# Gated linear attention into a squared-ReLU FFN: output sums scaled in PSUM and copied by ScalarE, turns placed one by one

## The chip, the cores and the metric

The kernel runs on 1 core of one Trainium2 chip. The metric is the device time of one execution in microseconds (us); less is better. Times named here are medians of several runs, or belong to one execution that was recorded by the profiler.

## The reference

The first part is a recurrent attention with a gate, the second a feed-forward network with a squared ReLU. Everything is float32.

```python
def _attn_ref(q, k, v, alpha):             # (4, 8, 768, 48) each
    for t in range(S):
        state = alpha[:, :, t, :, None] * state + np.einsum('bhd,bhe->bhde', k[:, :, t], v[:, :, t])
        y[:, :, t] = np.einsum('bhd,bhde->bhe', q[:, :, t], state)

x = attn_out.transpose(0, 2, 1, 3).reshape(3072, 384)
h = np.maximum(x @ w_in, 0.0)              # w_in (384, 2048)
out = (h * h) @ w_out                      # w_out (2048, 384)
```

## The kernel before

**Attention.** The 768 steps of each of the 4 batches are cut into 6 chunks of 128; a chunk of one batch, with its 8 heads, is a block, and there are 24 blocks. Blocks are worked on in pairs, named by the even block (`n0`): logarithms of alpha (`ln`, ScalarE), split of these into two parts (`sp`, VectorE), running sums over the chunk (`cs`, TensorE), exponentials of the sums (`eb`, `ei`, ScalarE), products with q and k (`mq`, `mk`, VectorE), the turn of both products (`turn`, 32 transposes for each block of TensorE into PSUM, then `kc`, `qc`, ScalarE copies), then `ga` and `gb` (scores, state sums, masks, states, and the outputs of an older pair), and at last the copies of the attention output into `x` (`ev_part`, ScalarE).

**FFN.** Four blocks make a group of 512 tokens, so there are 6 groups, `g` = 0 to 5. The first layer has 16 hidden tiles of 128 x 512 (`in_x`, `in_y`, `in_post`), the second sums 16 hidden tiles into 4 output tiles of 128 x 384 (`out_x`, `out_y`). Group 0 does most of its work in plain float32 (`ffn_in`, `out_plain`). From then on every factor is split in three: a scaled coarse part `a` or `b`, a remainder `l` and a difference `d`. Two passes, `b` times `a` and `l` times `l`, are summed in PSUM with the factor E = 2**-12 pending, and the third, `d` times `d`, is added. So a result is the first sum times (1 + E) plus the `d` pass.

For a hidden tile there are three ways to do that, one letter each in `tp` (in `tp1` for group 1). With `D`, ScalarE copies the first sum times E to `hid` (L754), VectorE adds PSUM after the `d` pass (L663) and squares with the ReLU (L771). With `M` and `A`, ScalarE scales the sum inside PSUM by 1 + E (L756) and the `d` pass is summed on top; then ScalarE does the ReLU (L776), and VectorE (`M`) or ScalarE (`A`) the square. For an output tile there is one way in groups 1 to 5: ScalarE copies the first sum times E to `osb` (L872), and VectorE adds PSUM to it after the `d` pass, and the store follows on SP's queue.

The weights' parts are made by `prepare`: `cast_w` on ScalarE, `rest_w` and `diff_w` on VectorE; `keep` stores the parts in DRAM, and `pump` fetches them again for each later group, all on SP's queue. `split_h` and `diff_h` split the hidden tiles; `splits_of_x` asks for the split of the next group's x.

**Order.** All engines run their own queue in order. The order is written by a weave: the FFN's steps are units with a cost, the attention's steps and the preparation of the weights are events with a time in the same units, and an event is put ahead of the first unit that starts at its time or later. The table `AT` holds these times; `base[g]` is where a group starts. `g0`, `g1`, `g2`, `g` list the pairs of each group: time, pair, whether it closes an older pair, whether it starts one, and for some a time at which `ga` and `gb` of the pair are done together (`joined`). `o0`, `o2`, `w_first`, `w_in_at`, `w_in_by` place the preparation of weights, `d_at` and `d_by` the differences of the output weights, `ahead` says how many steps ahead of their use the hidden tiles are split. The first 39 us follow the list `first`, which is written out.

`pads` and `places` put `align(place)` into TensorE's code: no-ops up to the slot `place` of a block of 256 instructions, at a time in a group or ahead of a pair's turn.

Of the kernel before, what the change touches and what calls it, by code (L numbers as in the profile page):

```python
# [12 lines left out]
AF = mybir.ActivationFunctionType  # L13
# [2 lines left out]


GB = 4
AT = {'v_by': (5.25, 6.24, 17.64), 'before': 2.2, 'places': ((4, 202), (16, 181)), 'pads': ((1, 9.0, 122), (1, 16.5, 223), (1, 33.0, 11), (2, 6.5, 120), (2, 21.0, 109)), 'evs': 0.65, 'lead': 4, 'lead1': 4, 'post': 3, 'w_first': (49.63, 28.64, 58.58), 'wstep': 0.45, 'd_at': 36.74, 'd_by': 0.95, 'w_in_at': 2.6, 'w_late': 1.45, 'w_in_by': 3.8, 'room1': 22, 'room': 25, 's0': 4, 'ahead': 5, 'xs': 0.2, 'g0': ((3.75, 4, False, True, 27.75), (21.38, 6, True, True), (27.75, 8, True, False)), 'sc0': (2.35, 2.35, 2.35), 'g1': ((1.38, 8, False, True, 15.62), (15.62, 10, True, True), (29.23, 12, True, False)), 'g2': ((0.56, 12, False, True), (19.11, 14, True, True), (32.13, 16, True, True)), 'g': ((1.71, 6, True, True), (17.38, 8, True, True)), 'g1x': 48.74, 'g2x': 49.24, 'gx': 46.88, 'g0x': 56.38, 'k0': 2, 'h0': 14, 'h1by': 2, 'evs0': 0.3, 'tp': 'ADMD', 'tp1': 'MMAD', 'split': 8, 'o0': (48.99, 50.24), 'o2': (17.75, 26.12, 26.5, 29.0, 30.61, 34.99), 'str1': 25.13, 'ga': 9.5, 'gb': 13.0, 'cv0': 1.5, 'first': 'ln0 warm0 cs0 load0v load2a ei0 load1v eb0 mk0 ln1 fill1 fill1 kT0 cs1 kc0 eb1 mq0 qT0 mq1 ei1 qc0 fill1 mk1 fill1 lt0 sc0 lt1 kT1 kv0 qT1 am0 ln2 weights2 us0 load2q kc1 qc1 cs2 sc1 fill1 am1 load2k ei2 load3a eb2 load4a fill1 kv1 st0 first0 us1 fill1 middle0 ln3 mq2 load3k ya0 qT2 yb0 mk2 fill1 qc2 kT2 cs3 kc2 load3q load2v weights5 sc2 eb3 load3v fill1 sga0 sgb0 fill1 ei3 ev0 mq3 mk3 am2 fill1 late0 qT3 kT3 sgc0 first1 kc3 qc3 middle1 kv2 ha0 sc3 us2 kv3 sga1 ha1 am3 us3 sgb1 load4k ya2 load4q load4v first2 yb2 late0 sgc1 middle2 weights6 ev2 lt3 lt2 st2 ha3 ha2 sgb2 sga2 hb1 sgc2 hb0 hb2 weights1 st1 hb3 st3 weights0', 'd3': 3.0}


RUN = {0: 128, 32: 32, 64: 64, 96: 32}
# [3 lines left out]
def kernel(  # L26
# [12 lines left out]
    nc = tc.nc  # L39
    B, H, S, D = q.shape  # L40
    C = 128
    NCH = S // C
    NP = H // 2
    NBLK = B * NCH
    DM, DF = moe_w_in.shape
# [49 lines left out]
    for x, n in (("q", 2), ("q", 3), ("k", 3)):  # L95
        t = lent[x, n] = two_k("qk_lent", shape=(H, 64))
# [144 lines left out]
    last = consts.tile([128, 4, NP], FP32, name="last")  # L241
# [36 lines left out]

    SPLIT = AT["split"]

# [361 lines left out]
    E = 2.0**-12  # L642
    NEAR = 1.0 - 2.0**-13
    acc = {}
# [8 lines left out]
    here, todo, room = {}, [], [22]  # L653
# [4 lines left out]
    def scaled_sum(out, x, scale, op, z):  # L658
        nc.vector.scalar_tensor_tensor(out=out, in0=x, scalar=scale, in1=z, op0=ALU.mult, op1=op)  # L659
# [7 lines left out]
    def lasting(w, p):  # L667
        return w == "o" and p < NW - AT["k0"]

# [9 lines left out]
    def keep(x, w, p):  # L679
        nc.sync.dma_start(out=kept_parts[x, w, p], in_=words(here[x, w, p]))  # L680
        stored.add((x, w, p))

    def rest_w(w, p):
        l = here["l", w, p] = wt("wl", FP32R, shapes[w])
        scaled_sum(l, whole[w][p], 1.0 / E, ALU.subtract, here["b", w, p].bitcast(FP32))
        cut.add((w, p))
        keep("l", w, p)

    def diff_w(w, p):
        l = here["l", w, p]  # L690
        d = here["d", w, p] = here.pop(("l", w, p)) if lasting(w, p) else wt("wd", FP32R, shapes[w])
        scaled_sum(d, here["b", w, p].bitcast(FP32), -E, ALU.add, l.bitcast(FP32))
        keep("d", w, p)
        pump()

    def prepare(at, w, p, late=0, diff_at=None):
        step = AT["wstep"]
        fs = (cast_w, rest_w, diff_w)
        out = [(at + i * step + late * (i > 1), f, (w, p)) for i, f in zip((0, 1, AT["d3"]), fs)]
        return out if diff_at is None else out[:-1] + [(diff_at, diff_w, (w, p))]  # L700

    def pump():
        while todo and todo[0] in stored and len(here) + 2 * NW - len(cut) < room[0]:
# [60 lines left out]
    kinds, g_now = [""], [0]  # L764
# [74 lines left out]
    def new_out(t):  # L839
        if t % 2 == 0:  # L840
            acc["out", t // 2] = cv_pool.tile([128, 2, DM], FP32, tag="upper", name="osb")
        return out_tile(t)
# [13 lines left out]
    def out_x(n, ns):  # L856
        p, jj = divmod(n, 2)
        a, l = h_parts.pop(n)
        for t in range(GB):
            if n == ns[0]:  # L860
                new_sum(t)
            of_tile(t, a, here["b", "o", p][:, jj], start=n == ns[0])
            of_tile(t, l, here["l", "o", p][:, jj], stop=n == ns[-1])
            if n == ns[-1]:
                x = acc[t][:, 0:DM]
                if len(ns) < NJ:
                    o = out_tile(t)
                    nc.vector.scalar_tensor_tensor(
                        out=o, in0=x, scalar=E, in1=o, op0=ALU.mult, op1=ALU.add
                    )  # L870
                else:
                    nc.scalar.activation(out=new_out(t), in_=x, func=AF.Copy, scale=E)  # L872
        if jj:
            used("l", "o", p)

    def out_y(g, ps, t, last):
        for p in ps:
            for n in (2 * p, 2 * p + 1):
                of_tile(
                    t, h_diff[n], here["d", "o", p][:, n % 2], stop=last and n == 2 * ps[-1] + 1  # L880
                )
        if last:
            o = out_tile(t)
            combine(((o, acc.pop(t)[:, 0:DM], ALU.add, o),))
            store(g, t, o)
        if t == GB - 1:
            for p in ps:
                h_diff.pop(2 * p)
                h_diff.pop(2 * p + 1)
                used("d", "o", p)  # L890
# [48 lines left out]
            hid[j] = two_k("hid")  # L939
        nc.scalar.activation(out=hid[j][:, cols], in_=r, func=AF.Square)  # L940

    def store(g, t, o):
        c, b = divmod(g * GB + t, B)
        r0 = (b * NCH + c) * C
        nc.sync.dma_start(out=out[r0 : r0 + C, :], in_=o)


    steps = {f.__name__: f for f in (ln, sp, cs, eb, ei, mq, mk, bl, br, lt, qT, qc, kT, kc, ev)}
# [19 lines left out]
    first = AT["first"]  # L968
    for word in first.split():
        f = max((x for x in steps if word.startswith(x)), key=len)  # L970
# [25 lines left out]
    places = dict(AT["places"])  # L996
# [5 lines left out]
    def attention(t, n0, after, scale=1, begun=True, whole_at=None, turn_at=None):  # L1002

        out = []
        old = n0 - 2 if after else None
        given = old, n0 if begun and n0 < NBLK else None

        def loads(at, *which):
            out.extend((at, load, (m, x)) for m, x in which if m < NBLK)

        for at, fs in EARLY if n0 < SPLIT else PLAN:
            for f in fs.split():
                w = t + (AT[f] if scale == 1 and f in ("ga", "gb") else at) * scale
                if f in ("ga", "gb") and whole_at is not None:
                    w = whole_at
                if f in ("turn", "kc0", "kc1", "qc0", "qc1") and turn_at is not None:
                    w = turn_at + (at - 6.5) * scale
                if f == "ga":
                    out.append((w, ga if whole_at is None else joined, given))
                elif f == "gb":  # L1020
                    if whole_at is None:
                        out.append((w, gb, given))
                    if after:
                        for p in range(NP):
                            out.append((w + AT["evs" if scale == 1 else "evs0"] * p, ev_part, (old, p)))
                if not begun:
                    continue
                if f == "ga":
                    loads(w, (n0 + 3, "k"))
                elif f == "gb":  # L1030
                    loads(w + AT["v_by"][0], (n0 + 2, "v"))
                    loads(w + AT["v_by"][1], (n0 + 3, "v"))
                    loads(w + AT["v_by"][2], (n0 + 4, "k"))
                elif n0 >= NBLK:
                    continue
                elif f == "turn":
                    if n0 in places:
                        out.append((w - AT["before"], align, (places[n0],)))
                    out.append((w, turn, (n0,)))
                    loads(w, (n0 + 2, "q"), (n0 + 3, "q"))  # L1040
                else:
                    n = n0 + int(f[-1])
                    out.append((w, steps[f[:-1]], (n,)))
                    if f[:-1] == "cs":
                        loads(w, (n + 2, "a"))
        return sorted(out, key=lambda x: x[0])
# [12 lines left out]
    NG = NBLK // GB  # L1059
# [38 lines left out]
    cv0 = AT["cv0"]  # L1098
# [11 lines left out]
    for g in range(1, NG):  # L1110
# [5 lines left out]
        if g + 1 < NG:  # L1116
            for t, n0, after, run, *other in AT["g1"] if g == 1 else AT["g2"] if g == 2 else AT["g"]:
                n0 = n0 if g < 3 else n0 + GB * g
# [46 lines left out]
```

## Time and profile before

| | |
|---|---|
| median of 3 runs | 520.47 us (519.84 to 520.86) |
| the profiled execution, its own time | 522.12 us |
| its span | 520.3 us |
| TensorE busy | 509.2 us (98%) |
| VectorE busy | 371.3 us (71%) |
| ScalarE busy | 308.8 us (59%) |

The span runs from the first to the last instruction of the profiled execution; its own time includes what lies around it. PE is TensorE's matmuls, PEld its weight loads (they overlap), DVE is VectorE, ACT ScalarE, POOL GpSimd, SP the engine whose queue issues most transfers. L739 is line 739 of the kernel. In a group of instructions, `o<-wd,hd 128x384 x288` means 288 instructions that write the tile `o` from `wd` and `hd`; what follows the bar is their busy time in us and the mean of one in ns, and after the next bar the idle time of the engine ahead of them with the engine and line that ended it.

### The profile page before, as it was taken

What the parts mean: (1) busy time and instruction counts of PE and PEld (TensorE: products, weight loads), DVE (VectorE), ACT (ScalarE), POOL (GpSimd) and SP (SyncE); (2) the same over time, 40 slices, a digit from 0 to 9 for tenths busy, and PEclk for the clock granted to TensorE, in tenths of its full rate; (3) what the DMA queues carried; (4) which work ended last, traced back from release to release, by engine and by line L of the source; (5) the groups of instructions that cost most, each with busy time, mean ns of one, the idle gap of its engine ahead of it and who ended that gap; (6) DMA issues with size and microseconds to landing.
All of it is one profiled execution on the core that took longest, in us unless ns stands there. A gap on an engine that the chain in (4) does not pass through costs nothing.

```text
span 520.3 us, 13238 instructions
## 1 busy us (share of the span) xinstructions
PE 509.2 (98%) x5382; PEld 427.1 (82%) x5382; DVE 371.3 (71%) x641; ACT 308.8 (59%) x656; POOL 32.4 (6%) x77
## 2 busy tenths in 40 slices
PE   8889999999999999999999999999999999999997
PEld 6666446669887999888998987899988899988996
DVE  3887979998997996776993566696465476363961
ACT  5577995676978656465663665954266855164620
POOL 4000202000102000010101020000000000000000
PEclk9999999999999999999999999999999999999999
DMA  9889776616889548799765689866673534798101
GB/s 174 179 241 272 216 184 143 177 33 229 246 241 199 168 116 295 251 263 274 201 169 144 205 241 266 228 171 183 234 250 124 185 121 154 274 332 301 64 1 60
DMA packets 133884, 101.58 MB, mean 195 GB/s; under 512 B 104640, under 2 KB 107712, under 8 KB 133824
## 3 DMA queue, kind: packets, MB, share of 16 engines
q1 hardware_dynamic: 132288, 100.68, 67.5%
q8 instruction: 43, 0.70, 0.6%
q0 software_dynamic: 1536, 0.05, 0.3%
q14 instruction: 17, 0.14, 0.1%
HBM read 83.39 MB, written 17.33 MB: 194 GB/s over the span
## 4 chain that ended last, share of the span: by engine, by line
PE 61%; DVE 4%; ACT 2%; DMA 1%; issue 0%; DVEq 0%
PE o L831 28%; PE h L739 26%; PE y L412 3%; PE T L590 1%; PE sckv L432 1%; PE sckv L460 1%; DVE wl L659 1%; ACT x L628 1%; DMA wl<-li 1%; ACT hx L714 1%; DVE hd L663 1%; DVE hl L659 0%; PE cs L300 0%; PE cs L301 0%; DVE q_in L316 0%
## 5 line engine op out<-in xcount | busy, mean ns | idle before, releaser
L739 PE MATMUL h<-xa,wb 128*128 128x512 f32 x240 | 68.5, 394 | 0.0
L739 PE MATMUL h<-xl,wl 128*128 128x512 f32 x240 | 67.7, 390 | 0.0
L739 PE MATMUL h<-xd,wd 128*128 128x512 f32 x240 | 67.0, 393 | 0.5 <-issue 0.5
L628 ACT COPY x<-y 32x256 f32<-32x256 f32 (+2 forms) x132 | 47.3, 365 | 24.9 <-PE y L412 22.4
L831 PE MATMUL o<-wb,ha 128*128 128x384 f32 x176 | 59.8, 340 | 0.0
L756 ACT ACTIVATE h<-h 128x512 f32<-128x512 f32 x44 | 25.8, 586 | 56.3 <-PE h L739 56.1
L831 PE MATMUL o<-wl,hl 128*128 128x384 f32 x176 | 58.9, 335 | 0.0
L831 PE MATMUL o<-wb,hx 128*128 128x384 f32 x160 | 54.2, 339 | 0.0
L831 PE MATMUL o<-wl,hx 128*128 128x384 f32 x160 | 53.6, 335 | 0.5 <-DVE hx L659 0.5
L663 DVE TENSOR_TENSOR hid<-h,hid 128x512 f32<-128x512 f32 x36 | 24.8, 688 | 40.0 <-PE h L739 37.2
L739 PEld LDWEIGHTS h<-xl,wl 128*128 128x128 f32 x240 | 45.0, 188 | 9.9 <-DVE xl L659 0.2
L739 PEld LDWEIGHTS h<-xd,wd 128*128 128x128 f32 x240 | 44.4, 188 | 9.8 <-issue 0.9
L739 PEld LDWEIGHTS h<-xa,wb 128*128 128x128 f32 x240 | 44.4, 188 | 9.2
L831 PE MATMUL o<-wd,hd 128*128 128x384 f32 x288 | 51.4, 335 | 0.0
L831 PEld LDWEIGHTS o<-wd,hd 128*128 128x128 f32 x288 | 49.9, 188 | 0.2
L931 PE MATMUL h<-x,w_in 128*128 128x512 f32 (+1 forms) x120 | 42.8, 510 | 1.5 <-DVE s L489 1.2
L754 ACT ACTIVATE hid<-h 128x512 f32<-128x512 f32 x36 | 21.6, 601 | 29.8 <-PE h L739 29.7
L714 ACT ACTIVATE ha<-hid 128x512 fp32r<-128x512 f32 x44 | 27.8, 639 | 18.6 <-DVE hx L659 8.2
L931 PEld LDWEIGHTS h<-x,w_in 128*128 128x128 f32 x120 | 22.5, 190 | 18.9 <-issue 15.1
L659 DVE SCALAR_TENSOR_TENSOR hl<-ha,hid 128x512 fp32r<-128x512 f32 x44 | 30.2, 686 | 7.1 <-ACT ha L714 7.1
L831 PEld LDWEIGHTS o<-wb,ha 128*128 128x128 f32 x176 | 33.0, 188 | 0.7
L831 PEld LDWEIGHTS o<-wl,hl 128*128 128x128 f32 x176 | 33.0, 188 | 0.3
(119 smaller groups left out, 922.8 us busy)
## 6 DMA issues: line engine op xcount, KB each, us to landing
wl<-lo SPq DMA_DIRECT2D x34, 384.0 KB, 4.5
wd<-do SPq DMA_DIRECT2D x34, 384.0 KB, 3.8
wl<-li SPq DMA_DIRECT2D x32, 384.0 KB, 4.3
wd<-di SPq DMA_DIRECT2D x32, 384.0 KB, 4.6
raw<-in_moe_w_in_dram SPq DMA_DIRECT2D x8, 768.0 KB, 6.8
raw<-in_moe_w_out_dram SPq DMA_DIRECT2D x8, 768.0 KB, 4.6
v_in<-in_v_dram SPq DMA_DIRECT2D x24, 192.0 KB, 4.5
out_dram<-osb SPq DMA_DIRECT2D x24, 192.0 KB, 2.0
```

The lines of the kernel that those rows point to most:

```text
L412: ins = nc.tensor.matmul(out=ys[e][64 * half : 64 * half + D + G * e, m % 2, p // 2, t], lhsT=lhsT, rhs=rhs, start=(half, e) not in seen, ...
L432: nc.tensor.matmul(out=ps[e][HALF[h], 0, p, :], lhsT=ks[rows, p, HALF[h]], rhs=qs[rows, p, HALF[h]], start=True, stop=True, skip_group_che ...
L460: nc.tensor.matmul(out=ps[h][64 * e : 64 * (e + 1), 1, p, G:64], lhsT=tile_of("k", n)[HALF[h], 2 * p + e, :], rhs=tiles["v"][n % NV][HALF[ ...
L628: copy(out=x[kk][to : to + m, t : t + 2], in_=blk[n]["y"][e][r : r + m, :, p // 2],)
L659: nc.vector.scalar_tensor_tensor(out=out, in0=x, scalar=scale, in1=z, op0=ALU.mult, op1=op)
L663: nc.vector.tensor_tensor(out=o, in0=x, in1=z, op=op)
L714: nc.scalar.activation(out=a, in_=x, func=AF.Copy, scale=E * NEAR)
L739: nc.tensor.matmul(out=acc["h", j], lhsT=here[w, "i", p][:, kk, jj * 128 : (jj + 1) * 128], rhs=x_parts[x][:, kk], start=start and kk == 0 ...
L754: nc.scalar.activation(out=hid[j], in_=x, func=AF.Copy, scale=E)
L756: nc.scalar.activation(out=x, in_=x, func=AF.Copy, scale=1.0 + E)
L831: nc.tensor.matmul(out=acc[t][:, 0:DM], lhsT=lhs[:, t * C : (t + 1) * C], rhs=rhs, start=start, stop=stop, skip_group_check=True,)
L931: nc.tensor.matmul(out=ps, lhsT=w[:, kk, c0 : c0 + 128], rhs=xT[g][kk][:, cols], start=(kk == 0), stop=(kk == KM - 1),)
```

## The change

- **Output sums.** A letter for each group, `'oa': 'DAAADA'`. In groups with `A` (1, 2, 3 and 5) ScalarE scales an output tile's first sum inside PSUM by 1 + E, the `d` pass is summed on top, and ScalarE copies the finished tile to `osb`. Groups 0 and 4 stay as they were.
- **The last tile** of group 5 is copied and stored in two halves of 192 columns: VectorE's half is stored by SP's queue, ScalarE's by ScalarE's own.
- **Turns.** `td` shifts the turn of each pair and its copies by a time of its own.
- **Stores of weight parts.** `keep` becomes an event of its own, `sd` later than the part that it stores (0.49 for `l`, 0 for `d`).
- **The table.** Most times of `AT` move, `tp1` goes from MMAD to MMMA, `ahead` from 5 to 4, `h0` from 14 to 16, five pads become four at other slots. The list `first` and the rest of `AT` stay.

The entries of `AT` (one line in the file) are shown one below the other, as far as they differ and are spoken of here:

```diff
-'places': ((4, 202), (16, 181))
+'places': ((4, 208), (16, 148))
-'pads': ((1, 9.0, 122), (1, 16.5, 223), (1, 33.0, 11), (2, 6.5, 120), (2, 21.0, 109))
+'pads': ((1, 33.0, 1), (2, 6.0, 96), (2, 21.0, 96), (2, 40.38, 27))
-'w_first': (49.63, 28.64, 58.58), 'wstep': 0.45, 'd_at': 36.74, 'd_by': 0.95
+'w_first': (50.38, 31.39, 60.45), 'wstep': 0.4, 'd_at': 39.24, 'd_by': 1.8
-'w_in_at': 2.6, 'w_late': 1.45, 'w_in_by': 3.8, 'ahead': 5
+'w_in_at': 1.98, 'w_late': 3.08, 'w_in_by': 4.05, 'ahead': 4
-'g1': ((1.38, 8, False, True, 15.62), (15.62, 10, True, True), (29.23, 12, True, False))
+'g1': ((1.25, 8, False, True, 14.62), (17.5, 10, True, True), (25.23, 12, True, False))
-'g2': ((0.56, 12, False, True), (19.11, 14, True, True), (32.13, 16, True, True))
+'g2': ((2.81, 12, False, True), (19.11, 14, True, True), (32.13, 16, True, True))
-'g': ((1.71, 6, True, True), (17.38, 8, True, True)), 'g1x': 48.74, 'tp1': 'MMAD'
+'g': ((1.83, 6, True, True), (18.5, 8, True, True)), 'g1x': 47.74, 'tp1': 'MMMA'
-'o0': (48.99, 50.24), 'o2': (17.75, 26.12, 26.5, 29.0, 30.61, 34.99), 'str1': 25.13
+'o0': (48.74, 50.99), 'o2': (17.88, 22.12, 28.13, 30.5, 32.36, 34.12), 'str1': 18.5
+'td': (0.0, 0.0, 0.26, 0.12, 0.12, -0.19, 0.0, 0.44, -0.37, -0.5, 0.06, 0.0), 'sd': (0.49, 0.0), 'oa': 'DAAADA'
```

```diff
@@ rest_w, diff_w, prepare
-        keep("l", w, p)
...
+    def keep_d(w, p):
         keep("d", w, p)
         pump()
...
+        whens = (
+            (at, cast_w, (w, p)), (at + step, rest_w, (w, p)), (diff_at, diff_w, (w, p)),
+            (at + step + AT["sd"][0], keep, ("l", w, p)), (diff_at + AT["sd"][1], keep_d, (w, p)),
+        )
@@ out_x, after the last of the two passes
+                elif AT["oa"][g_now[0]] == "A":
+                    nc.scalar.activation(out=x, in_=x, func=AF.Copy, scale=1.0 + E)
                 else:
                     nc.scalar.activation(out=new_out(t), in_=x, func=AF.Copy, scale=E)
@@ out_y
-        if last:
+        if last and g and AT["oa"][g] == "A":
+            o, x = new_out(t), acc.pop(t)[:, 0:DM]
+            if g < NG - 1 or t < GB - 1:
+                nc.scalar.activation(out=o, in_=x, func=AF.Copy)
+                store(g, t, o)
+            else:
+                for copy, cols in ((nc.vector.tensor_copy, slice(0, DM // 2)), (nc.scalar.copy, slice(DM // 2, DM))):
+                    copy(out=o[:, cols], in_=x[:, cols])
+                    store(g, t, o, cols)
+        elif last:
             o = out_tile(t)
             combine(((o, acc.pop(t)[:, 0:DM], ALU.add, o),))
             store(g, t, o)
@@ store
+        ask = nc.scalar if cols.start else nc.sync
+        ask.dma_start(out=out[r0 : r0 + C, cols], in_=o[:, cols])
@@ attention
+        later = AT["td"][n0 // 2] if n0 < NBLK else 0
...
+                if f in ("turn", "kc0", "kc1", "qc0", "qc1"):
+                    w += later
```

More of the change, by code (lines that the diff above doesn't have):

```diff
@@ L18 @@
 GB = 4
-AT = {'v_by': (5.25, 6.24, 17.64), 'before': 2.2, 'places': ((4, 202), (16, 181)), 'pads': ((1, 9.0, 122), (1, 16.5, 223), (1, 33.0, 11), (2, 6.5, 120), (2, 21.0, 109)), 'evs': 0.65, 'lead': 4, 'lead1': 4, 'post': 3, 'w_first': (49.63, 28.64, 58.58), 'wstep': 0.45, 'd_at': 36.74, 'd_by': 0.95, 'w_in_at': 2.6, 'w_late': 1.45, 'w_in_by': 3.8, 'room1': 22, 'room': 25, 's0': 4, 'ahead': 5, 'xs': 0.2, 'g0': ((3.75, 4, False, True, 27.75), (21.38, 6, True, True), (27.75, 8, True, False)), 'sc0': (2.35, 2.35, 2.35), 'g1': ((1.38, 8, False, True, 15.62), (15.62, 10, True, True), (29.23, 12, True, False)), 'g2': ((0.56, 12, False, True), (19.11, 14, True, True), (32.13, 16, True, True)), 'g': ((1.71, 6, True, True), (17.38, 8, True, True)), 'g1x': 48.74, 'g2x': 49.24, 'gx': 46.88, 'g0x': 56.38, 'k0': 2, 'h0': 14, 'h1by': 2, 'evs0': 0.3, 'tp': 'ADMD', 'tp1': 'MMAD', 'split': 8, 'o0': (48.99, 50.24), 'o2': (17.75, 26.12, 26.5, 29.0, 30.61, 34.99), 'str1': 25.13, 'ga': 9.5, 'gb': 13.0, 'cv0': 1.5, 'first': 'ln0 warm0 cs0 load0v load2a ei0 load1v eb0 mk0 ln1 fill1 fill1 kT0 cs1 kc0 eb1 mq0 qT0 mq1 ei1 qc0 fill1 mk1 fill1 lt0 sc0 lt1 kT1 kv0 qT1 am0 ln2 weights2 us0 load2q kc1 qc1 cs2 sc1 fill1 am1 load2k ei2 load3a eb2 load4a fill1 kv1 st0 first0 us1 fill1 middle0 ln3 mq2 load3k ya0 qT2 yb0 mk2 fill1 qc2 kT2 cs3 kc2 load3q load2v weights5 sc2 eb3 load3v fill1 sga0 sgb0 fill1 ei3 ev0 mq3 mk3 am2 fill1 late0 qT3 kT3 sgc0 first1 kc3 qc3 middle1 kv2 ha0 sc3 us2 kv3 sga1 ha1 am3 us3 sgb1 load4k ya2 load4q load4v first2 yb2 late0 sgc1 middle2 weights6 ev2 lt3 lt2 st2 ha3 ha2 sgb2 sga2 hb1 sgc2 hb0 hb2 weights1 st1 hb3 st3 weights0', 'd3': 3.0}
@@ new lines @@
+AT = {'v_by': (5.25, 8.24, 17.64), 'before': 2.2, 'places': ((4, 208), (16, 148)), 'pads': ((1, 33.0, 1), (2, 6.0, 96), (2, 21.0, 96), (2, 40.38, 27)), 'evs': 0.65, 'lead': 4, 'lead1': 4, 'post': 3, 'w_first': (50.38, 31.39, 60.45), 'wstep': 0.4, 'd_at': 39.24, 'd_by': 1.8, 'w_in_at': 1.98, 'w_late': 3.08, 'w_in_by': 4.05, 'room1': 22, 'room': 25, 's0': 4, 'ahead': 4, 'xs': 0.2, 'g0': ((4.75, 4, False, True, 27.75), (21.13, 6, True, True), (27.12, 8, True, False)), 'sc0': (2.35, 2.35, 2.35), 'g1': ((1.25, 8, False, True, 14.62), (17.5, 10, True, True), (25.23, 12, True, False)), 'g2': ((2.81, 12, False, True), (19.11, 14, True, True), (32.13, 16, True, True)), 'g': ((1.83, 6, True, True), (18.5, 8, True, True)), 'g1x': 47.74, 'g2x': 48.62, 'gx': 48.26, 'g0x': 55.38, 'k0': 2, 'h0': 16, 'h1by': 2, 'evs0': 0.3, 'tp': 'ADMD', 'tp1': 'MMMA', 'split': 8, 'o0': (48.74, 50.99), 'o2': (17.88, 22.12, 28.13, 30.5, 32.36, 34.12), 'str1': 18.5, 'ga': 9.5, 'gb': 13.0, 'cv0': 1.5, 'first': 'ln0 warm0 cs0 load0v load2a ei0 load1v eb0 mk0 ln1 fill1 fill1 kT0 cs1 kc0 eb1 mq0 qT0 mq1 ei1 qc0 fill1 mk1 fill1 lt0 sc0 lt1 kT1 kv0 qT1 am0 ln2 weights2 us0 load2q kc1 qc1 cs2 sc1 fill1 am1 load2k ei2 load3a eb2 load4a fill1 kv1 st0 first0 us1 fill1 middle0 ln3 mq2 load3k ya0 qT2 yb0 mk2 fill1 qc2 kT2 cs3 kc2 load3q load2v weights5 sc2 eb3 load3v fill1 sga0 sgb0 fill1 ei3 ev0 mq3 mk3 am2 fill1 late0 qT3 kT3 sgc0 first1 kc3 qc3 middle1 kv2 ha0 sc3 us2 kv3 sga1 ha1 am3 us3 sgb1 load4k ya2 load4q load4v first2 yb2 late0 sgc1 middle2 weights6 ev2 lt3 lt2 st2 ha3 ha2 sgb2 sga2 hb1 sgc2 hb0 hb2 weights1 st1 hb3 st3 weights0', 'd3': 3.0, 'td': (0.0, 0.0, 0.26, 0.12, 0.12, -0.19, 0.0, 0.44, -0.37, -0.5, 0.06, 0.0), 'sd': (0.49, 0.0), 'oa': 'DAAADA'}
@@ L697, in prepare @@
         step = AT["wstep"]
-        fs = (cast_w, rest_w, diff_w)
-        out = [(at + i * step + late * (i > 1), f, (w, p)) for i, f in zip((0, 1, AT["d3"]), fs)]
-        return out if diff_at is None else out[:-1] + [(diff_at, diff_w, (w, p))]
+        if diff_at is None:
+            diff_at = at + AT["d3"] * step + late
+        whens = (
+            (at, cast_w, (w, p)), (at + step, rest_w, (w, p)), (diff_at, diff_w, (w, p)),
+            (at + step + AT["sd"][0], keep, ("l", w, p)), (diff_at + AT["sd"][1], keep_d, (w, p)),
+        )
+        return list(whens)
     def pump():
@@ L940, in ffn_in, with store @@
         nc.scalar.activation(out=hid[j][:, cols], in_=r, func=AF.Square)
-    def store(g, t, o):
+    def store(g, t, o, cols=slice(0, None)):
         c, b = divmod(g * GB + t, B)
         r0 = (b * NCH + c) * C
-        nc.sync.dma_start(out=out[r0 : r0 + C, :], in_=o)
+        ask = nc.scalar if cols.start else nc.sync
+        ask.dma_start(out=out[r0 : r0 + C, cols], in_=o[:, cols])
     steps = {f.__name__: f for f in (ln, sp, cs, eb, ei, mq, mk, bl, br, lt, qT, qc, kT, kc, ev)}
```

## The prediction

> **What bounds the kernel now.** I read the page first, then the busy time by stretches, then the timeline where TensorE (PE) stops, and last the groups of instructions for prices.
>
> ```profile
> span 520.3 us, 13238 instructions
> PE 509.2 (98%) x5382; PEld 427.1 (82%) x5382; DVE 371.3 (71%) x641; ACT 308.8 (59%) x656; POOL 32.4 (6%) x77
> ...
> q8 instruction: 43, 0.70, 0.6%
> ```
>
> PE is busy 509.2 of 520.3 us, so the kernel is bound by its matmuls, and the diff adds or removes none. What can move is the 11.1 us of idle PE. The busy time by stretches shows where it lies (columns: window, length, busy PE, weight loads, VectorE, ScalarE, GpSimd, then granted clock, DMA share, GB/s):
>
> ```profile
> 0.00:39.00 39.00, 33.77 (x609) 25.84 (x610) 25.50 (x53) 24.60 (x55) 5.32 (x29) 1.00 0.94 198
> ...
> 156.00:169.00 13.00, 12.34 (x79) 9.46 (x77) 10.24 (x20) 11.00 (x26) 3.37 (x6) 1.00 0.93 199
> ...
> 182.00:195.00 13.00, 12.54 (x158) 11.79 (x157) 12.41 (x21) 7.12 (x15) 0.00 (x0) 1.00 0.47 113
> ...
> 273.00:286.00 13.00, 12.40 (x238) 11.32 (x236) 5.06 (x11) 3.95 (x12) 2.35 (x4) 1.00 0.57 144
> ...
> 312.00:325.00 13.00, 12.50 (x291) 10.09 (x291) 7.86 (x17) 7.26 (x17) 0.00 (x0) 1.00 1.04 267
> ...
> 507.00:520.30 13.30, 9.63 (x56) 9.31 (x54) 2.23 (x4) 0.00 (x0) 0.00 (x0) 1.00 0.17 59
> ```
>
> The start loses 5.2 us and the end 3.7 us; four stretches between lose 0.66, 0.46, 0.60 and 0.50 us, together all 11.1. The start follows the list `first`, which the diff leaves word for word, so I count nothing there. A matmul's end is modelled, so idle time understates a stall. I measure each stall from start to start and take off what the same instructions need undisturbed, from the chain of waits (the last three rows):
>
> ```profile
> 157.29 0.34 PE L300 MATMUL cs<-hi,causal_r 128*128 128x384 f32 x1
> 157.47 0.34 PE L301 MATMUL cs<-lo,causal_r 128*128 128x384 f32 x1
> ...
> 158.53 0.85 PE L739 MATMUL h<-xd,wd 128*128 128x512 f32 x3
> ...
> 163.40 0.46 PE L590 MATMUL T<-ident,k_in 64*128 64x64 f32 x8
> 165.14 0.46 PE L590 MATMUL T<-ident,q_in 64*128 64x64 f32 x8 [0.51 <-DVE q_in L316]
> 165.53 0.96 PE L739 MATMUL h<-xa,wb 128*128 128x512 f32 x3
> ...
> 187.44 0.34 PE L831 MATMUL o<-wb,hx 128*128 128x384 f32 x1
> 188.23 0.44 PE L831 MATMUL o<-wl,hx 128*128 128x384 f32 x1 [0.46 <-DVE hx L659]
> ...
> 273.19 0.46 PE L590 MATMUL T<-ident,k_in 64*128 64x64 f32 x8
> 274.14 0.46 PE L590 MATMUL T<-ident,q_in 64*128 64x64 f32 x8 [0.50 <-DVE q_in L316]
> 275.47 0.44 PE L831 MATMUL o<-wb,hx 128*128 128x384 f32 x1
> ...
> 317.96 0.84 PE L739 MATMUL h<-xl,wl 128*128 128x512 f32 x3
> 319.30 0.50 PE L739 MATMUL h<-xd,wd 128*128 128x512 f32 x1 [0.50 <-issue]
> ...
> 221.40 1.16 PE T L590 x32
> 424.09 26.55 PE o L831 x152
> 450.64 32.68 PE h L739 x144
> ```
>
> - Sums of logs of pair 10 (blocks 10 and 11): four matmuls from 157.29 to 158.53, 1.24 us, against 4 x 0.18 (the step from 157.29 to 157.47): 0.52 us lost.
> - Turn of pair 10: 163.40 to 165.53 is 2.13 us against 1.16 for 32 transposes: 0.97 lost, for VectorE's product `q_in`.
> - Output of group 1: 187.44 to 188.23 is 0.79 against 26.55/152 = 0.175: 0.62 lost, for VectorE's split `hx`.
> - Turn of pair 16: 273.19 to 275.47 is 2.28 against 1.16: 1.12 lost, again for `q_in`.
> - Group 3: 317.96 to 319.30 is 1.34 against 3 x 32.68/144 = 0.68: 0.66 lost to "issue", so to nothing that the profile shows.
>
> That is 3.89 us in five places, four of them waits for VectorE.
>
> **The change part by part.** Prices of the instructions that change engine:
>
> ```profile
> L663 DVE TENSOR_TENSOR osb<-o,osb 128x384 f32<-128x384 f32 x24 | 13.2, 555 | 27.9 <-PE o L831 23.1 <-DMA wl<-li 4.0
> L872 ACT ACTIVATE osb<-o 128x384 f32<-128x384 f32 x20 | 8.2, 496 | 28.8 <-PE o L831 28.8
> L754 ACT ACTIVATE hid<-h 128x512 f32<-128x512 f32 x36 | 21.6, 601 | 29.8 <-PE h L739 29.7
> L756 ACT ACTIVATE h<-h 128x512 f32<-128x512 f32 x44 | 25.8, 586 | 56.3 <-PE h L739 56.1
> L776 ACT ACTIVATE hid<-h 128x512 f32<-128x512 f32 x44 | 26.6, 609 | 0.0
> L663 DVE TENSOR_TENSOR hid<-h,hid 128x512 f32<-128x512 f32 x36 | 24.8, 688 | 40.0 <-PE h L739 37.2 <-ACT hid L754 2.7
> L771 DVE SCALAR_TENSOR_TENSOR hid<-hid 128x512 f32<-128x512 f32 x36 | 24.7, 687 | 0.3
> L663 DVE TENSOR_TENSOR hid<-hid 128x512 f32<-128x512 f32 x24 | 16.3, 685 | 4.4 <-ACT hid L776 4.4
> ```
>
> *Output sums.* In groups 1, 2, 3 and 5, 16 adds leave VectorE: 16 x 0.555 = 8.9 us. ScalarE's 16 scaled copies become 16 scalings inside PSUM (586 ns in PSUM against 601 out of it at 512 columns: the same price), and 16 plain copies come on top: 15.5 x 0.496 = 7.7 us. PE waits for ScalarE before the `wd` matmuls as it did before (then it could not overwrite what was being read, now it needs what is written), so that wait keeps its length. The copies wait in ScalarE's queue for PE's last matmul of each tile; behind them stand the next group's first scalings, which need later matmuls anyway, at most 4 x 0.496 = 2 us of ScalarE at a group's change. PE waits for none of the adds today, so on the path this part is worth nothing by itself.
>
> *Group 1's kinds, MMAD to MMMA.* Four hidden tiles of 16 change from D to M. VectorE gives up 0.688 + 0.687 and takes 0.685, so 0.69 each, 2.8 us in all; ScalarE pays 0.586 + 0.609 - 0.601 = 0.59 each, 2.4 us. This relieves VectorE in the group where three of the five stalls are.
>
> *Pair 10.* One schedule unit is 6 x 0.227 / 1.05 = 1.3 us. The joined attention step ahead of it goes from 15.62 to 14.62 and the pair's own start from 15.62 to 17.5, with the turn 0.19 earlier. Between that step and the turn there were 6.5 units; now there are 9.2, so VectorE has 2.7 units = 3.5 us more for the same queue (masks, states, splits of logs, products, and the weight splits that stay near unit 18.3). The two stalls there were 0.52 + 0.97 = 1.5 us. I take back 0.5 and 0.85.
>
> *Group 1's output.* The six `wd` splits of the output weights move from 36.74 to 41.5 to 39.24 to 48.24, so four of them leave the stretch where VectorE was busy 12.41 of 13 us. I take back 0.5 of the 0.62. The last now stands at 48.24, behind the next group's three first splits of x at 47.74, and PE wants it near 49.4 (the second layer's three-pass steps end at 25.28 + 16 x 1.08 = 42.6, three pairs of 4 x 0.54 units follow, then half a tile): it could be late by half a unit, 0.65 us.
>
> *Pair 16.* Its start stays at 32.13, its turn moves 0.37 units (0.5 us) earlier, which by itself lengthens the wait. But `ahead` 4 for 5 queues the splits of h one output step later, and one of these stood between the products:
>
> ```profile
> 272.14 0.68 DVE L659 SCALAR_TENSOR_TENSOR hl<-ha,hid 128x512 fp32r<-128x512 f32 x1
> 272.93 0.69 DVE L663 TENSOR_TENSOR hd<-ha,hl 128x512 fp32r<-128x512 f32 x1
> 273.54 0.55 DVE L316 TENSOR_TENSOR q_in<-q_in,b 128x384 f32<-128x384 f32 x1
> ```
>
> From 272.14 to 273.54 is 1.4 us. With that pair behind `q_in` the wait of 1.12 goes and 0.5 may come back; if it stays in front, 0.5 is added. I take back 0.55 (bounds -0.5 and 1.12).
>
> *Places and pads.* These fill the code with no-ops up to a slot of a 256-instruction block. Two times 5382 instructions over 43 fetches is 250 for each, so a fetch of 0.70/43 MB brings one block.
>
> ```profile
> L1000 PEldq NOP  x102: 13/13/13, 57.0 to 267.9; - x102
> ```
>
> Seven pads cost 102 no-ops of 13 ns, 15 on average, and six will cost about as many: at pair 4 the slot moves by 6, just the three weight loads and three matmuls of one more step ahead of it. What the new slots bring to the one "issue" stall no row can tell: between 0 and 0.66; I take 0.3. The Trainium skill, "Runtime: NRT & Kernel Launch", section "Instruction fetch mechanics", has blocks of 256 instructions fetched while the last one runs, and calls the cost of crossing mostly hidden. The 43 fetches agree on the size; by that rule the stall would be no fetch, the pads would bring 0, and the gain would be 0.3 us less.
>
> *Stores of split weights* (`sd`) are asked for 0.49 units = 0.64 us later on SP's queue, so the loads behind them wait less for VectorE; no stall today is a wait for a load after 39 us. I count 0. The loads of q move with each turn by at most half a unit and count 0 too. The other turns had no stall to lose; shifts up to 0.5 units could make one of 0.3 us or so.
>
> *The last tile.*
>
> ```profile
> 516.74 0.56 DVE L663 TENSOR_TENSOR osb<-o,osb 128x384 f32<-128x384 f32 x1 [2.23 <-PE o L831]
> ...
> out_dram<-osb SPq DMA_DIRECT2D x24, 192.0 KB, 2.0
> ```
>
> Two engines copy 192 columns each. Half of 0.56 is 0.28; a fixed part makes it rather 0.36, so 0.2 us is won (0 to 0.28). Both halves' stores then land in the time of one, 2.0 us. Were a store's time in proportion to its bytes, halves would win 1.0 us more. "DMA: Bandwidth & Descriptors" of the Trainium skill, section "Anatomy of one DMA — SWDGE (gpsimd) path", speaks against that: about 2.0 us of a transfer is fixed, bytes come on top. The row of 2.0 us for 192 KB agrees; by that rule the win stays 0.2.
>
> **The sum.** 0.5 + 0.85 + 0.5 + 0.55 + 0.3 + 0.2 = 2.9 us. I give back 0.4 for the late `wd` split and small waits of moved turns: 2.5 us. The profiled execution took 522.1 us with its span of 520.3, and the runs' median is 520.47; I take the same 2.5 us off each: span 517.8, median 518.0. With every stall and the tail gone it is 4.1 us, 516.4; the bounds of the unknowns at their worst (no gain at pair 16 but 0.5 lost, no fetch, no tail, 0.65 for the late split) leave 0.5 + 0.85 + 0.5 - 0.5 - 0.65 = 0.7 us, 519.8.
>
> **The rivals.**
> *The waits only move (520.2).* VectorE's queue in group 1 is nearly full, and its stalls come back at pair 14's turn or in the output. For it: 12.41 of 13 us busy. Against it: 2.8 us of work leaves there and four `wd` splits go later. Only tail and chance remain, 0.2 us.
> *A pad is passed by one slot (about 521.8, slower).* Then up to 255 no-ops run, 255 x 13 ns = 3.3 us, in PE's own queue and too long for the matmuls queued ahead to hide. It decides where the instructions ahead of a pad differ by one from what its slot allows for. With a thin gain of 2.0 in the stalls that is 520.5 + 3.3 - 2.0 = 521.8. Against it: the pair 4 slot, which moves by just one step's 6.
> *ScalarE becomes late in group 1 (519.2).* It was busy 11.00 of 13 us near pair 10 and gets 2.4 us more in that group. If half of it shows as late scalings, the gain falls by 1.2 us.
>
> **How the numbers follow.** Forecast 0.57, ScalarE late 0.12, waits only move 0.16, pad passed 0.15. A measurement of this kernel tells apart about 0.2%, 1.04 us: faster is below 519.4, slower above 521.5. The forecast case gives faster for all but its worst corner (0.55), ScalarE late gives 0.11 of its 0.12; same takes the moved waits and what is left, 0.18 with a part of the pads; slower has the rest of the pads and new waits, 0.16. The range goes from the sum with all stalls gone, rounded to 516.0, to 521.6 inside the pad case.
>
> **What would show it.** Right: the transposes of pairs 10 and 16 run in about 1.2 us, four `cs` matmuls in 0.7, `wl,hx` in group 1 without a VectorE wait; the last copy under 0.4 us; about 100 no-ops. Wrong: over 200 no-ops; "DVE" waits of PE at a turn as long as before; PE waiting for ScalarE's `h` in group 1, or for `wd` at the end of its output.

## The result: 2.5 us faster, mostly from group 1 of the schedule

The changed kernel takes 517.38 us (median of 5 runs, 517.07 to 518.01) against 519.84 us for the kernel before (5 runs, 519.16 to 520.86). The ratio is 0.9951, 95% interval 0.9936 to 0.9967: 2.5 us less, between 1.7 and 3.3. The forecast was 518.0 us and 2.5 us less.

The page of the changed kernel, its two first lines:

```profile
span 515.4 us, 13223 instructions
PE 507.9 (99%) x5382; PEld 427.4 (83%) x5382; DVE 361.0 (70%) x622; ACT 318.3 (62%) x676; POOL 32.5 (6%) x77
```

The span fell by 4.9 us, twice what the runs say. The stages tell why: I took the start of the first matmul of each stage, and of PE's last matmul, from both traces, and the differences between them.

| stage | before, us | after, us |
|---|---|---|
| start, to the first full `h<-x,w_in` | 43.55 | 41.40 |
| group 0, to group 1's first `h` | 84.80 | 84.71 |
| group 1 | 81.88 | 79.88 |
| group 2 | 85.08 | 85.14 |
| group 3 | 79.98 | 79.15 |
| group 4 | 75.18 | 75.37 |
| group 5, to PE's last matmul | 65.81 | 65.81 |
| from there to the end | 4.04 | 3.90 |

The start took between 41.40 and 43.55 us in the 14 profiles of this case, whichever kernel it was, so 2.1 us of the difference between the two profiles belong to the run. The other stages mostly repeat to a few hundredths where the program is the same (the changed kernel's second profile differs by at most 0.04 in each), and they sum to 2.8 us: 2.0 in group 1, 0.8 in group 3. Group 3 of the kernel before is the exception: three kernels below that keep its table there (`pair10_alone`, `pair10_new_slots`, `wd_late_alone`) took 79.26, 79.79 and 79.54 us for it, so between 0.1 and 0.8 us of that stage belong to the change.

The busy time by stretches, over the same work as the prediction's rows (columns as there):

```profile
153.00:166.00 13.00, 13.00 (x86) 10.80 (x85) 10.69 (x18) 12.67 (x29) 3.38 (x6) 1.00 0.75 206
...
182.00:195.00 13.00, 13.00 (x190) 12.30 (x189) 11.86 (x18) 10.15 (x26) 0.00 (x0) 1.00 0.51 138
269.00:282.00 13.00, 12.48 (x248) 11.43 (x251) 6.15 (x13) 3.93 (x12) 2.35 (x4) 1.00 0.64 156
310.00:323.00 13.00, 13.00 (x207) 10.79 (x198) 6.92 (x16) 7.69 (x19) 0.00 (x0) 1.00 0.77 218
```

PE is now busy throughout the three stretches in which it lost 0.66, 0.46 and 0.50 us. One place is left, at 269 us, and it is the only row in the list of PE's waits between 100 and 510 us (in total, times, longest):

```profile
PE T L590 <- DVE q_in L316: 0.5, 1, 0.5
```

The timeline of PE shows pair 10's sums without a gap (157.09 to 157.80 is 0.71 us for four, 0.53 less than before), pair 10's turn in 1.16 us (162.69 to 163.85), and pair 16's turn with the same gap as before:

```profile
157.09 0.34 PE L300 MATMUL cs<-hi,causal_r 128*128 128x384 f32 x1
...
157.80 0.86 PE L746 MATMUL h<-xd,wd 128*128 128x512 f32 x3
...
162.69 0.46 PE L590 MATMUL T<-ident,k_in 64*128 64x64 f32 x8
...
163.85 1.67 PE L746 MATMUL h<-xd,wd 128*128 128x512 f32 x6
...
268.97 0.46 PE L590 MATMUL T<-ident,k_in 64*128 64x64 f32 x8
269.94 0.46 PE L590 MATMUL T<-ident,q_in 64*128 64x64 f32 x8 [0.51 <-DVE q_in L316]
...
271.27 0.44 PE L838 MATMUL o<-wb,hx 128*128 128x384 f32 x1
```

### The profile page after: what moved, and what is told of

It reads as the page before. It is cut to its first block, busy times and chain, and to the rows that moved or that the text cites. A ratio compares the mean times of both kernels' runs of the same rounds, so it can differ in the third digit from the quotient of the medians.

```text
span 515.4 us, 13223 instructions
## 1 busy us (share of the span) xinstructions
PE 507.9 (99%) x5382; PEld 427.4 (83%) x5382; DVE 361.0 (70%) x622; ACT 318.3 (62%) x676; POOL 32.5 (6%) x77
## 4 chain that ended last, share of the span: by engine, by line
PE 95%; DVE 2%; ACT 2%; issue 0%; POOL 0%; DVEq 0%; ACTq 0%; POOLq 0%
PE o L838 39%; PE h L746 32%; PE h L949 8%; PE y L412 4%; PE sckv L432 3%; PE T L590 2%; PE sckv L460 2%; PE cs L297 1%; ACT x L628 1%; PE warm L251 1%; PE zeros L398 1%; DVE x L628 0%; PE cs L300 0%; PE cs L301 0%; PE kT L368 0%
## 5 line engine op out<-in xcount | busy, mean ns | idle before, releaser
L763 ACT ACTIVATE h<-h 128x512 f32<-128x512 f32 x48 | 28.2, 587 | 38.9 <-PE h L746 38.9
L663 DVE TENSOR_TENSOR hid<-h,hid 128x512 f32<-128x512 f32 x32 | 22.0, 689 | 36.8 <-PE h L746 36.8
L761 ACT ACTIVATE hid<-h 128x512 f32<-128x512 f32 x32 | 19.2, 601 | 29.1 <-PE h L746 29.1
L721 ACT ACTIVATE ha<-hid 128x512 fp32r<-128x512 f32 x44 | 27.8, 639 | 13.4 <-DVE hl L659 7.0
L443 DVE COPY_PREDICATED am<-halves_mask,sckv 128x256 f32<-128x256 uint32 x48 | 18.6, 440 | 21.7 <-PE sckv L460 18.3
```

The lines of the kernel that those rows point to most:

```text
L443: nc.vector.copy_predicated(out=am_h(n)[:, e, n % 2], data=ps[e][:, 0], mask=halves_mask.bitcast(U32).unsqueeze(1).to_broadcast([128, NP, ...
L663: nc.vector.tensor_tensor(out=o, in0=x, in1=z, op=op)
L721: nc.scalar.activation(out=a, in_=x, func=AF.Copy, scale=E * NEAR)
L761: nc.scalar.activation(out=hid[j], in_=x, func=AF.Copy, scale=E)
L763: nc.scalar.activation(out=x, in_=x, func=AF.Copy, scale=1.0 + E)
```

## The experiments

All times are medians; each kernel was compared with the kernel before on the same chip, where that took 519.8 to 520.3 us.

### Parts taken back from the changed kernel

`adds_back`: all output sums as before, with VectorE's adds.

```diff
-'oa': 'DAAADA'
+'oa': 'DDDDDD'
```

> The changed kernel with all output sums made as before ('oa' all D), so the halved last tile goes too. Theory (the schedule of group 1 brings the gain, the moved adds nothing on the path): 2.3 us below the kernel before, only the 0.15 us of the last tile lost; group 1 takes 79.9 us from its first h to group 2's first h, as in the changed kernel. Rival (VectorE's relief of 8.9 us is what removed the stalls): at most 1.5 us below, with VectorE waits of PE in groups 1 to 3.

517.85 us, ratio 0.9964 (0.9952 to 0.9977), and the stages say it more finely: group 1 takes 79.87 us, every other stage is the changed kernel's to 0.03 us, and only the end is longer, 4.04 for 3.90. Taking 8.9 us of adds off VectorE shortened nothing but the last tile. In the kernel before, group 1's adds run at 208 to 213 us, behind its three waits.

`kinds_back`: group 1's hidden tiles as before.

```diff
-'tp1': 'MMMA'
+'tp1': 'MMAD'
```

> The changed kernel with group 1's kinds back at MMAD. Theory (3.5 us more room ahead of pair 10's turn suffices by itself): within 0.4 us of the changed kernel. Rival (the 2.8 us that leave VectorE in group 1 are needed): a wait for hx or q_in returns in group 1 and the gain falls by 0.5 to 1.5 us.

517.76 us, ratio 0.9957 (0.9945 to 0.9969); group 1 takes 79.82 us against 79.88. The new kinds do nothing for the time either, though 2.8 us leave VectorE there. Adds and kinds were taken back one at a time, not together.

`whole_last_tile`: the very last tile copied whole by ScalarE, stored in one piece.

```diff
-            if g < NG - 1 or t < GB - 1:
+            if True:
```

> The changed kernel with the very last tile copied whole by ScalarE and stored in one piece. Theory: 0.15 to 0.2 us above the changed kernel, read from PE's last matmul to the end of the span: 3.9 us there, about 4.05 here. Rival (two half stores land sooner than one whole): 0.4 us or more above.

518.08 us, 0.9965 (0.9953 to 0.9977). From PE's last matmul to the end it is 3.89 us, as with halves, so neither theory held: the halves bring nothing. The changed kernel's timeline shows why:

```profile
511.84 0.36 DVE L898 COPY osb<-o 128x192 f32<-128x192 f32 x1 [13.53 <-PE o L838]
512.22 0.33 SPq L964 DMA_DIRECT2D out_dram<-osb  x1
512.23 0.32 ACT L898 COPY osb<-o 128x192 f32<-128x192 f32 x1 [2.68 <-DVE osb L898]
512.58 0.38 ACTq L964 DMA_DIRECT2D out_dram<-osb  x1
```

ScalarE waits for VectorE's half, and the copies run one after the other, 0.36 + 0.32 us, longer than ScalarE's whole copy (0.49 us, the mean of 15). The trace names VectorE's copy as what ended the wait, not the reason. Both copies read one PSUM tile and both write `osb`; since the store of VectorE's half (512.22) reads `osb` while ScalarE writes the other half, the read of PSUM is the likelier reason. "PSUM — Partial Sum Buffer" of the Trainium skill, section "PSUM bank collisions raise a hardware error", says that two engines must not access one bank in the same partitions at the same time, two reads included; this trace agrees as far as it shows them one behind the other.

The halves are ready some 0.2 us later than the whole, and their stores land some 0.2 us faster (1.65 to 1.7 us from request to landing for 96 KB, 1.85 for 192 KB at this place), so nothing is left. The 0.14 us that the changed kernel gains on the kernel before are had by the whole copy too: ScalarE's 0.49 in place of VectorE's 0.56, and a start that is 0.07 us sooner behind the last matmul.

### One part alone in the kernel before

`pair10_alone`: only the entries of group 1's pairs.

```diff
-'g1': ((1.38, 8, False, True, 15.62), (15.62, 10, True, True), (29.23, 12, True, False))
+'g1': ((1.25, 8, False, True, 14.62), (17.5, 10, True, True), (25.23, 12, True, False))
```

> The kernel before with only the three entries of g1 changed (joined step at 14.62, pair 10 at 17.5, the closing step at 25.23). Theory: the stalls at cs and at the turn of pair 10 (0.52 + 0.97 us) go, the wait for hx stays: 1.5 us below the kernel before. Rival (they come back as later waits for VectorE in the output of group 1): under 0.5 us below, with a longer wait for hx.

519.29 us, ratio 0.9989 (0.9980 to 0.9999): 0.5 us less, not 1.5. All three waits of group 1 are gone, the one for `hx` too, but a new stop stands at 173 us, and it names no engine:

```profile
172.92 0.34 PE L831 MATMUL o<-wb,hx 128*128 128x384 f32 x1
174.72 0.44 PE L831 MATMUL o<-wl,hx 128*128 128x384 f32 x1 [1.46 <-issue]
```

Group 1 takes 81.46 us against 81.88. I read the 1.6 us as a late fetch of code and tried new slots.

`pair10_new_slots`: the same, and of group 1's three pads only one, at the changed kernel's slot.

```diff
-'pads': ((1, 9.0, 122), (1, 16.5, 223), (1, 33.0, 11), (2, 6.5, 120), (2, 21.0, 109))
+'pads': ((1, 33.0, 1), (2, 6.5, 120), (2, 21.0, 109))
```

> The kernel before with the three entries of g1 changed and, of the pads of group 1, only one left, at 33.0 with slot 1, as in the changed kernel. Theory (the g1 entries alone remove all three waits for VectorE in group 1, 2.1 us, and 1.6 us of it were lost to a late fetch of code at 173 us): group 1 from its first h to group 2's first h takes 79.8 us, as in the changed kernel, against 81.5 with the old pads; the time is 2.0 to 2.8 us below the kernel before. Rival (the 1.6 us are a wait for the weights' parts, which the changed kernel prepares earlier): group 1 takes 81.5 again.

519.86 us, 0.9990 (0.9981 to 0.9998); group 1 takes 81.38 us. My theory fell. The stop for "issue" shrinks to 0.2 us of idle (0.4 from start to start), and most of the time is lost to VectorE instead, 3 us later (1.0 from start to start):

```profile
175.46 0.34 PE L831 MATMUL o<-wb,hx 128*128 128x384 f32 x1 [0.22 <-issue]
...
178.11 1.00 PE L432 MATMUL sckv<-qs,ks 48*64 48x64 f32 x29 [0.81 <-DVE us L473]
```

So this is the first rival of the prediction, at work in the half-made change: the waits of pair 10 move to a later one. In `pair10_alone` VectorE ran the same instructions as late, and the stop for "issue" stood in front of that wait. What the rest of the change does about it can be seen in VectorE's timeline, this kernel above, the changed one below:

```profile
174.61 0.68 DVE L771 SCALAR_TENSOR_TENSOR hid<-hid 128x512 f32<-128x512 f32 x1
175.21 1.82 DVE L659 SCALAR_TENSOR_TENSOR wl<-w_out,wb 128x768 fp32r<-128x768 f32 x2
176.95 0.77 DVE L443 COPY_PREDICATED am<-halves_mask,sckv 128x256 f32<-128x256 uint32 x2
177.61 0.35 DVE L473 TENSOR_TENSOR us<-sckv,s 128x192 f32<-128x192 f32 x1
```

```profile
172.39 0.69 DVE L663 TENSOR_TENSOR hd<-hx 128x512 fp32r<-128x512 f32 x1
173.00 0.77 DVE L443 COPY_PREDICATED am<-halves_mask,sckv 128x256 f32<-128x256 uint32 x2
173.66 0.35 DVE L473 TENSOR_TENSOR us<-sckv,s 128x192 f32<-128x192 f32 x1
...
174.78 0.95 DVE L659 SCALAR_TENSOR_TENSOR wl<-w_out,wb 128x768 fp32r<-128x768 f32 x1
```

Two remainders of output weights and a square, 2.5 us of VectorE, stand ahead of the masks and sums that PE waits for. In the changed kernel one of the two is made 4 units earlier (`o2`, 22.12 for 26.12), and the other stands behind the sums (28.13 for 26.5). The square is gone there by the new kinds, without which group 1 was as short (`kinds_back`). That `o2` is what group 1's gain needs beside `g1` fits both traces, but it was not run by itself; which entries suffice stays open.

`wd_late_alone`: only the differences of the output weights later.

```diff
-'d_at': 36.74, 'd_by': 0.95
+'d_at': 39.24, 'd_by': 1.8
```

> The kernel before with only d_at 39.24 and d_by 1.8, so that four of the six wd splits leave the output steps. Theory: the wait for hx near 187 us (0.62 us) goes, the two at pair 10 stay: 0.6 us below the kernel before. Rival (that wait is decided by what VectorE does earlier, or the last wd is late at the end of group 1): 0 to 0.5 us above.

519.78 us, 0.9999 (0.9990 to 1.0009). Group 1 takes 81.85 us, and PE waits as before; this is the list of its waits between 100 and 510 us:

```profile
PE T L590 <- DVE q_in L316: 1.0, 2, 0.5
PE o L831 <- DVE hx L659: 0.5, 1, 0.5
```

The rival held: the wait for `hx` is made by what VectorE does before, not by the differences near it. This list shows one more thing: its code is placed as in the kernel before, with the same 102 no-ops, but the "issue" row of group 3 is not in it. From start to start the stop there measures 0.14 us instead of 0.66.

### Where the code's blocks begin

`slot16_moved`: the kernel before with 40 no-ops more ahead of pair 16's turn.

```diff
-'places': ((4, 202), (16, 181))
+'places': ((4, 202), (16, 221))
```

> The kernel before with the slot ahead of pair 16's turn at 221 instead of 181: 40 no-ops more, and all later borders of code blocks 40 instructions earlier; nothing else moves. Theory (the 0.66 us to 'issue' in group 3 is a late fetch of code): that stall goes or sits at another instruction; 0.6 us below the kernel before if it goes, and the 40 no-ops (0.52 us) stay behind the matmuls. Rival (it is a wait that the profile cannot name): the stall stays at the same matmul, the time is the same or 0.5 us more.

526.16 us (522.99 to 528.32), ratio 1.0108 (1.0083 to 1.0132): 5.6 us slower by the ratio, for 40 no-ops. The old stop near 318 us is gone. In its place the waits of PE list new ones (each row: in total, times, longest):

```profile
PE y L412 <- issue: 1.8, 1, 1.8
...
PE h L739 <- issue: 0.4, 1, 0.4
...
PE o L831 <- issue: 0.3, 1, 0.3
```

The profiled execution (522.99 us) was the shortest of the six, and its stages are 2.6 us longer than those of the kernel before; what the others lose beyond that no profile shows. For five stops named "issue" I looked up the packets of the code's own queue (q8) in the trace, times in us:

```
kernel            code packet starts   takes   PE goes on   from start to PE
before                   316.43        1.45      319.30         2.9
pair10_alone             172.18        1.11      174.72         2.5
slot16_moved             312.64        1.35      315.19         2.6
slot16_moved             341.04        1.00      343.60         2.6
slot16_moved             394.72        1.03      396.99         2.3
```

Every stop ends 2.3 to 2.9 us after a code packet started, and the matmul behind it waits for no semaphore. The count of instructions agrees. The stop of the kernel before comes 653 pairs of weight load and matmul behind the first transpose of pair 16's turn, the first stop of `slot16_moved` 633, so 40 instructions sooner, just as far as the borders moved. From its first stop to its second are 768 instructions (378 pairs and 12 for semaphores), from there to its third 1024 more (504 pairs and 16): 3 and 4 blocks of 256. So these are late fetches: the first part of the theory held, the 0.6 us did not. Where matmuls are short, a block is used up sooner, as the chain of waits of the kernel before has it:

```profile
226.90 0.62 PE sckv L432 x32
```

With their weight loads these are 64 instructions in 0.62 us; at that rate, an estimate, a block of 256 would last 2.5 us, no longer than a fetch takes. The Trainium skill ("Runtime: NRT & Kernel Launch", "Instruction fetch mechanics") calls the cost of crossing blocks mostly hidden; here it is mostly, but the exceptions cost up to 2.0 us.

`pad_passed`: the changed kernel with one pad's slot just behind the code's place, so that it fills nearly a whole block.

```diff
-(2, 21.0, 96)
+(2, 21.0, 60)
```

> The changed kernel with the pad at 21.0 in group 2 set to slot 60, which the code has passed there: 220 no-ops more at that pad and 36 more at the next slot. Theory of the rival in the prediction (no-ops of a passed pad are paid): 256 x 13 ns = 3.3 us above the changed kernel, less what the matmuls already queued hide (at most about 0.5 us). Against it: if PE's queue hides them, under 1 us.

534.12 us, ratio 1.0262 (1.0249 to 1.0275). Against the changed kernel it loses some 16 us, not 3.3. 256 more no-ops ran than in the changed kernel with its 81 (337), and 234 of them in a row at this pad (count, recorded length in ns, start of the first and of the last in us):

```profile
L1019 PEldq NOP  x234: 13/13/13, 234.8 to 252.1; - x117
```

Each is recorded with 13 ns, but they start 74 ns apart on average, and 233 such steps are 17.3 us. PE lived on queued matmuls until 238.9 and then stood still, first in the timeline, then in the busy time by stretches:

```profile
238.06 0.84 PE L746 MATMUL h<-xd,wd 128*128 128x512 f32 x3
252.30 1.62 PE L746 MATMUL h<-xa,wb 128*128 128x512 f32 x3 [13.40 <-issue]
```

```profile
238.00:252.00 14.00, 0.90 (x4) 0.40 (x3) 2.84 (x6) 1.08 (x2) 0.00 (x0) 0.70 0.40 99
252.00:256.00 4.00, 3.70 (x10) 3.15 (x11) 0.00 (x0) 0.71 (x2) 0.00 (x0) 0.50 0.00 0
```

PE went on 0.2 us behind the last no-op, so this stop is the no-ops themselves and no late fetch, though the profile calls both "issue": the one code packet on the way started at 249.02, took 1.22 us and was there 2 us before PE went on. After the stop the granted clock was 0.50 for 4 us, so that three matmuls took 1.62 us instead of 0.84. The same 72 to 74 ns for a no-op stand in `slot16_moved`, whose 50 at one place took 3.6 us (265.5 to 269.1), all but 0.4 us behind queued matmuls.

`pads_gone`: the changed kernel without its four pads.

```diff
-'pads': ((1, 33.0, 1), (2, 6.0, 96), (2, 21.0, 96), (2, 40.38, 27))
+'pads': ()
```

> The changed kernel without its four pads; the slots ahead of the turns of pairs 4 and 16 stay. Theory (the pads keep the borders of code blocks out of stretches of short matmuls): new stops of PE for 'issue', each 0.5 to 2 us, 0.5 to 4 us above the changed kernel in all. Rival (the borders matter little, or the slots were chosen without effect): within 0.4 us of the changed kernel.

518.38 us, ratio 0.9966 (0.9953 to 0.9978), the same as the changed kernel within the intervals, and PE lists no "issue" after 100 us. So this kernel does not need its pads; but a wrong slot costs more than the whole change brings. Its one wait there, 0.6 us in group 2, is listed for ScalarE's `b`, but PE goes on 0.1 us behind the last of 38 no-ops ahead of pair 16's turn; the turn then waits less, and group 2 takes 85.11 us, as in the changed kernel. Whether the new slot ahead of pair 16's turn or the moved code took the stop out of group 3 was not run.

### A better version, and the changed kernel again

`turn16_later` and `turn16_again`: pair 16's turn one output step later, its slot moved with it.

```diff
-'places': ((4, 208), (16, 148))
+'places': ((4, 208), (16, 164))
-'td': (..., 0.44, -0.37, -0.5, ...)
+'td': (..., 0.44, 0.71, -0.5, ...)
```

> The changed kernel with the turn of pair 16 one output step later (td 0.71 for -0.37, its slot 164 for 148, so that the no-ops stay as many). Theory (the turn comes 1.2 us ahead of VectorE's products): its wait goes, 1.0 to 1.2 us below the changed kernel. Rival (the wait moves on to the split of h or to the scores of pair 16): the same as the changed kernel within 0.4 us.

> The changed kernel once more, on the chip of the other runs of this call: 517.1 to 518.0 us, 2.5 us below the kernel before, with the same times between the stages to 0.1 us, but for the start, which differs by up to 2 us from run to run.

> The changed kernel with pair 16's turn one output step later, on the same chip as the changed kernel. Theory: 1.0 to 1.2 us below it, as the profile of the first run had it between the stages. Rival: the two cannot be told apart, under 0.4 us.

516.89 us, ratio 0.9938 (0.9925 to 0.9950), and again 517.26, 0.9937 (0.9924 to 0.9951). The changed kernel on the chip of the second run: 518.07, 0.9958 (0.9946 to 0.9971). The intervals of these ratios overlap, but the stages do not: group 2 takes 84.01 and 84.02 us with the later turn and 85.14 and 85.16 without. The turn then runs freely:

```profile
271.12 0.46 PE L590 MATMUL T<-ident,k_in 64*128 64x64 f32 x8
271.42 0.42 PE L590 MATMUL T<-ident,q_in 64*128 64x64 f32 x8
271.67 0.42 PE L590 MATMUL T<-ident,k_in 64*128 64x64 f32 x8
271.92 0.42 PE L590 MATMUL T<-ident,q_in 64*128 64x64 f32 x8
```

This is the fastest kernel of the case, 0.8 us below the changed one on the same chip by the medians, 1.1 by the stage.

## Why the prediction was right

The number came out: 2.5 us less were forecast and measured (517.4 for 518.0; the 0.6 us between these lie in the kernel before, which took 519.84 in place of 520.47). The larger part, group 1, came by the mechanism that it named, VectorE's queue ahead of pair 10. Three of the smaller terms were wrong, and that their errors cancel is luck. Of its signs of being wrong one showed, the wait at pair 16's turn.

- *Group 1, 0.5 + 0.85 + 0.5 expected.* All three waits went, 2.0 us in the stage. The reason held in part: more time for VectorE's queue ahead of pair 10. The step that failed is the price by parts: it gave the `hx` wait to the later `wd` splits, but these alone bring 0.0 us, and moving pair 10 alone removes all three waits and loses 1.6 us of the 2.1 again at a new one. The gain belongs to entries together, and which of them stays open. VectorE's relief by the kinds, named as support, could be taken back without a loss.
- *Pair 16, 0.55 expected.* Nothing came (1.12 us lost before, 2.30 - 1.16 = 1.14 after). The step that failed said that with `ahead` 4 the split would fall behind `q_in`: that pair of splits (`hl` and its `hd`) went back, but the pair ahead of it in VectorE's queue (`hx` and its `hd`) went back too and stood in its place:

```profile
267.47 0.55 DVE L316 TENSOR_TENSOR k_in<-k_in,inv 128x384 f32<-128x384 f32 x1
267.94 0.69 DVE L659 SCALAR_TENSOR_TENSOR hx<-hx,hid 128x512 fp32r<-128x512 f32 x1
268.73 0.69 DVE L663 TENSOR_TENSOR hd<-hx 128x512 fp32r<-128x512 f32 x1
269.34 0.55 DVE L316 TENSOR_TENSOR q_in<-q_in,b 128x384 f32<-128x384 f32 x1
```

- *The "issue" stop, 0.3 expected of 0.66.* Group 3 lost its stop and became 0.8 us shorter than in the one profile of the kernel before. That it was a late fetch is now shown by the packets and the count of instructions; that its size is 0.14 to 0.66 for the same placing of code was not foreseen, so this term cannot be sized from one profile.
- *The last tile, 0.2 expected.* 0.14 came, but not by two engines copying at once, which they did not do.
- *0.4 given back.* The late `wd` split did not happen. Group 4 gave back 0.2; where, no single stop shows.
- *The rivals.* ScalarE near pair 10 was busy 12.67 of 13 us and PE did not wait for it. The waits that only move appeared in `pair10_alone` and `pair10_new_slots`. A passed pad cost some 16 us: 3.3 was the wrong price, since it took the recorded 13 ns of a no-op for what it holds of PE's queue, which is 74 ns. Of the 17.3 us, 3.9 were hidden by queued matmuls, not 0.5. The changed kernel ran 81 no-ops, so its pads met their slots.

## What to carry to other kernels

When one engine is busy 98% of the span, list its stops from start to start and look for what stands ahead of the awaited instruction in the other engine's queue; reordering that queue can win the stop back, while relieving it of work elsewhere (8.9 us here) won nothing. One part of such an order moved alone may only move the wait, so read the stage, not the one stop. A stop that names no engine can be a late fetch of code or a run of no-ops, so look up both before you explain it. And before crediting an edit, subtract what differs from run to run: here the start, by up to 2.1 us.

## What the runs showed of the hardware that was not expected

- A stop of PE for code ends 2.3 to 2.9 us after the fetch's packet starts, and in `slot16_moved`, where it was counted, the stops stand whole blocks of 256 instructions apart. 40 no-ops that moved these borders cost 5.6 us, of which the profiled execution shows 2.6.
- A no-op recorded with 13 ns holds PE's queue for 74. 234 in a row took 17.3 us and stopped PE for 13.4, and the clock granted afterwards was 0.50 for 4 us.
- Half the bytes of a store save little: the last tiles' stores of 192 KB took 1.85 us from request to landing, its halves of 96 KB 1.65 and 1.7 us. So the fixed part of about 2.0 us that the prediction names is too large for these stores, which SP and ScalarE ask for: they take less than that as a whole.
